# Gram and masked products of a gated delta rule: one matmul of 128 columns per unit in place of two of 64, from the fourth group on

## The chip, the cores and the metric

The kernel runs on one core of a Trainium2 chip. The metric is the device time of one execution in microseconds; the median of three runs before the change is 651.9 us (651.75 to 652.64). A core has a matrix engine (TensorE, in the profile PE, with its weight loads as PEld), a vector engine (VectorE, DVE), a scalar engine (ScalarE, ACT), GpSimd (POOL) and a queue for DMAs (SP). Matmul results go to PSUM, which the vector and scalar engines read.

## The reference

Two parts follow each other. The first is a delta rule with a state of 48 x 48 for each of 4 batches and 8 heads, over 768 tokens; the second is a gated MLP on its output, with 384 model and 1536 inner columns.

```
k_n = k / (norm(k) + 1e-06)
for t in range(S):
    y[t] = q[t] @ state
    v_old = k_n[t] @ state
    state = state + beta[t] * outer(k_n[t], v[t] - v_old)
x = y as (3072 tokens, 384)
out = (sigmoid(x @ w_gate) * (x @ w_val)) @ w_out
```

Taken in chunks of 64 tokens, the first part needs for each chunk and head the products of all its keys with one another (K by K, the Gram matrix, from which the norms and a triangular system come) and of its keys with its queries (K by Q, masked to the past).

## The kernel before

**Groups and units.** A group is one chunk of 64 tokens of all 4 batches, 256 tokens; there are N = 12 groups, 0 to 11. In a group there are 32 units, one per batch and head. A unit is named by `e` (which half of the 128 partitions holds its keys), `x` (which kind of two) and `j` (0 to 7). The tile `kqp[g % 2]` holds, in six sections, a group's K (sections 0 and 1 for the two kinds), its Q (2 to 4) and the masked products (the free halves of 2 and 4, and section 5). There are two such tiles, so group g's data is loaded over that of group g-2 (`load_group`, lines 122 to 126: four DMAs of K and Q, then those of V, K by tokens and beta).

**The two products.** `gram(g)` (lines 282 to 309) issues 32 matmuls of K by K (line 291): 48 rows, 64 stationary and 64 moving columns, into two PSUM tiles of one bank each, one per `e`. Ten ScalarE copies bring the result into G (line 303, six copies in another order of axes) and L (line 308, four copies). `masked(g)` (lines 311 to 327) issues 32 matmuls of K by Q (line 319) into two PSUM tiles, and four VectorE multiplications by a mask (line 324) write them back into `kqp`. The four units of one `j` lie in four different quarters of the array, by the rows of K and the columns of the output. All these PSUM tiles come from the pool `ps_aux`, which has two banks; the products `pu` of the updates (line 475), `yy` of the rows (lines 501 and 504) and the transposes `pt` (line 540) take turns in it with them.

**What follows.** `norms(g)` (from line 235) transposes G on VectorE and works out the norms; `solve(g)` (from line 329) solves the triangular systems in 66 VectorE steps; then `rest`, `updates` in three steps, `rows`, `advance` and `flip` take the group through the state and hand its output to the MLP. In the first three groups a shorter solve, `solve_halves`, is used, which takes both aux banks for a moment.

**The MLP.** For each group and each of 12 slices of the inner columns there is a gate block (`gate_val`, line 559: 18 matmuls of 256 columns), a sigmoid on ScalarE (line 564), a product on VectorE (line 565), a split into two numbers of lower precision (lines 570 and 575), and an output block two slices later (`outp`, line 590: 6 matmuls of 384 columns). Group 0 uses other forms of these (lines 556 and 584).

**The order of the work.** The order on every engine is the order in which the program issues it. It goes by slots, two to a slice and W = 24 to a group: an even slot has a gate block, an odd one an output block.

```
def slot(s):
    (odd: outp; even: gate_val)
    for fn in plan[s]: fn()
    (odd: split_hi; even: split_lo, gated)
    for fn in late[s]: fn()
    for fn in tail[s]: fn()
```

Lists `plan` and `late` hold what the first part does in a slot; `tail` holds the preparation of weights in the first 44 slots (ScalarE line 212, VectorE line 219). With w = 24 (g - 1), group g has its data loaded in `plan` of slot w-27; Gram in `late` of slot w-18 (`gram_later`, copies in the three slots after it: 4, 2, 4); the masked products in `late` of slot w-12 (`mask_later`, two masks in that slot, two at the head of the next); norms and solve over slots w-14 to w+8; `rest` at w+6; the updates at w+10, w+12 and w+14; `rows` and `advance` at w+16; the transposes at w+18. Group 3 has Gram at slot 32 and the masked products at 36. Counted modulo 24, a period of the steady part has `rest` and Gram in slot 6, the second update and the masked products in slot 12.

The counter `busy` is the planner's estimate of what VectorE has to do in a slot besides the solve: `spread` deals the steps of norms and solve to the slots by `max(0.1, 1.6 - busy[s])`. `mask_later` adds 1.4 to each of two slots.

Of the kernel before, what the change touches and what calls it, by code (L numbers as in the profile page):

```python
# [12 lines left out]
F32 = mybir.dt.float32  # L13
# [6 lines left out]
ALU = mybir.AluOpType  # L20
# [3 lines left out]
B, H, S, D = 4, 8, 768, 48  # L24
C = 64
# [5 lines left out]
J = 8  # L31
CP = 2 * J
NQ = 4 * CP
KINDS = [(e, x) for x in range(2) for e in range(2)]


def tokens_at(e, x):
    return 64 * e if x else 64 - 64 * e
# [17 lines left out]
def deltanet_gated_mlp(ctx: ExitStack, tc: tile.TileContext, kd, qd, kv, beta, words, out):  # L56
    nc = tc.nc
# [4 lines left out]
    wk = ctx.enter_context(tc.tile_pool(name="wk", bufs=1))  # L62
    ps_seq = ctx.enter_context(tc.tile_pool(name="ps_seq", bufs=2, space=PSUM))
    ps_aux = ctx.enter_context(tc.tile_pool(name="ps_aux", bufs=2, space=PSUM))
# [5 lines left out]
    kqp = [const.tile([128, 6, J, C], F32, name=f"kqp{i}") for i in range(2)]  # L70
# [3 lines left out]
    pmask = const.tile([128, 2, C], F32, name="pmask")  # L74
# [9 lines left out]
    state = [{} for _ in range(N)]  # L84
# [197 lines left out]
    def gram(g):  # L282

        kq, st = kqp[g % 2], state[g]
        st["G"] = G = wk.tile([128, 32, CP], F32, name=f"G_{g}", tag="G", bufs=1)
        st["L"] = L = wk.tile([128, CP, 32], F32, name=f"L_{g}", tag="L", bufs=2)
        pg = [ps_aux.tile([128, J, C], F32, name=f"pg_{g}_{e}", tag="aux") for e in range(2)]
        for j in range(J):
            for e, x in KINDS:
                r, t = 64 * e, tokens_at(e, x)  # L290
                nc.tensor.matmul(out=pg[e][t:t + 64, j], lhsT=kq[r:r + D, x, j], rhs=kq[r:r + D, x, j], start=True, stop=True)  # L291
        return blocks_of(pg, G, L, g == 0)
# [18 lines left out]
    def masked(g):  # L311

        kq = kqp[g % 2]
        pool, tag = (ps_aux, "aux") if g else (ps_out, "po")
        pp = [pool.tile([128, J, C], F32, name=f"pp_{g}_{e}", tag=tag) for e in range(2)]
        for j in range(J):
            for e, x in KINDS:
                r, t = 64 * e, tokens_at(e, x)
                nc.tensor.matmul(out=pp[e][t:t + 64, j], lhsT=kq[r:r + D, x, j], rhs=kq[r:r + D, 3 if x else 2 + 2 * e, j], start=True, stop=True)  # L319

        def masks():
            for e, x in sorted(KINDS):
                t, sec = tokens_at(e, x), 5 if x else 2 + 2 * e
                nc.vector.tensor_tensor(out=kq[t:t + 64, sec], in0=pp[e][t:t + 64],  # L324
                                        in1=pmask[t:t + 64, e].unsqueeze(1).to_broadcast([64, J, C]), op=ALU.mult)
                yield
        return masks()

    def solve(g):

        st = state[g]
        gp, gam = st["gp"], st["gam"]
        X = wk.tile([128, 16, 32], F32, name=f"X_{g}", tag="X", bufs=1)

        def scale(lo, hi):
            nc.vector.scalar_tensor_tensor(out=gp[:, lo:hi, 0:hi], in0=gp[:, lo:hi, 0:hi], scalar=-1.0,
                                           in1=gam[:, 0:hi].unsqueeze(1).to_broadcast([128, hi - lo, hi]), op0=ALU.mult, op1=ALU.mult)
        nc.vector.tensor_tensor(out=X, in0=dmask, in1=gam.unsqueeze(1).to_broadcast([128, 16, 32]), op=ALU.mult)
        yield
        scale(16, 32)  # L340
        yield
        scale(0, 16)
        yield
        for j in range(31, 0, -1):
            k, n = j // 2, 16 - j // 2
            tmp = wk.tile([128, n, j], F32, name=f"tmp_{g}_{j}", tag="tmp", bufs=2)
            nc.vector.tensor_tensor(out=tmp, in0=X[:, k:16, j:j + 1].to_broadcast([128, n, j]),  # L347
                                    in1=gp[:, j:j + 1, 0:j].to_broadcast([128, n, j]), op=ALU.mult)
            yield
            nc.vector.tensor_tensor(out=X[:, k:16, 0:j], in0=X[:, k:16, 0:j], in1=tmp, op=ALU.add)  # L350
            yield
        nc.vector.transpose(mt.rearrange("q c (k r) -> q k c r", r=2), X.rearrange("q k (c r) -> q k c r", r=2))
        yield
# [78 lines left out]
    def rest(g):  # L432

        st = state[g]
        kq, V = kqp[g % 2], st["kv"][:, 1]
        st["pk"] = pk = [ps_seq.tile([128, J, D], F32, name=f"pk_{g}_{e}", tag="seq") for e in range(2)]
        if g == 0:
            for e in range(2):
                nc.tensor.matmul(out=pk[e].rearrange("q j d -> q (j d)"), lhsT=flat[:, 0:128], rhs=su[:, 2].rearrange("q j d -> q (j d)").bitcast(BF16)[:, 0:J * D],
                                 start=True, stop=True, skip_group_check=True)  # L440
        for j in range(J if g else 0):
            for e, x in KINDS:
                r, t = 64 * e, tokens_at(e, x)
                nc.tensor.matmul(out=pk[e][t:t + 64, j], lhsT=kq[r:r + D, x, j], rhs=su[r:r + D, 2 if x else e, j],  # L444
                                 start=j == 0, stop=True, skip_group_check=True)
        if g == 0:
            st["R"] = [V[:, e * J:(e + 1) * J] for e in range(2)]
        else:
            st["R"] = [wk.tile([128, J, D], F32, name=f"R_{g}_{e}", tag="row", bufs=3) for e in range(2)]
            less(g)  # L450
# [61 lines left out]
    def advance(g):  # L512

        if g == N - 1:
            return
        Kt = state[g]["kv"][:, 0]
        if 1:
            pd = [ps_seq.tile([128, J, D], F32, name=f"pd_{g}_{t}", tag="seq") for t in range(2)]
            for j in range(J):
                for e, x in KINDS:  # L520
                    r, t = 64 * e, tokens_at(e, x)
                    nc.tensor.matmul(out=pd[t // 64][r:r + D, j], lhsT=Kt[t:t + 64, e * J + j], rhs=su[t:t + 64, 3 if x else e, j], start=True, stop=True)  # L522
            for e, x in KINDS:
                r, t = 64 * e, tokens_at(e, x)
                sl = su[r:r + D, 2 if x else e]
                if g == 0:
                    nc.scalar.copy(sl, pd[t // 64][r:r + D])
                else:
                    nc.vector.tensor_tensor(out=sl, in0=sl, in1=pd[t // 64][r:r + D], op=ALU.add)  # L529
# [73 lines left out]
    plan = collections.defaultdict(list)  # L603
    late = collections.defaultdict(list)

    def steps(gen, n=1):
        def fn():
            for _ in range(n):
                next(gen, None)
        return fn  # L610
# [14 lines left out]
    def take(gen, n=1):  # L625
        for _ in range(n):
            next(gen, None)
# [91 lines left out]
    busy = collections.Counter()  # L719

    def mask_later(g, s):
        def fn():
            masks = masked(g)
            take(masks, 2)
            plan[s + 1].insert(0, steps(masks, 2))
        late[s].append(fn)
        for i in range(2):
            busy[s + i] += 1.4

    def gram_later(g, s):  # L730
        def fn():
            copies = gram(g)
            for i, n in enumerate((4, 2, 4)):
                plan[s + 1 + i].append(steps(copies, n))
        late[s].append(fn)

    solves = []
    for g in range(N):
        w = W * (g - 1)
        if g == 0:  # L740
            late[3].append(lambda: advance(0))
            continue
        up, at_rows = (13, 19) if g < 3 else (10, 16)
        at_rest = {1: 8, 2: 28}.get(g, w + 6)
        late[at_rest].append(lambda g=g: rest(g))
        for step in range(3):
            late[w + up + 2 * step].append(lambda g=g, step=step: updates(g, step))
        late[w + at_rows].append(lambda g=g: rows(g))
        late[w + at_rows].append(lambda g=g: advance(g))
        for c in range(2):  # L750
            late[w + at_rows + 2].append(lambda g=g, c=c: flip(g, c))
            busy[w + at_rows + 2] += 0.6
        busy[at_rest] += 1.1
        busy[w + up + 2] += 1.1
        busy[w + at_rows] += 1.1
        busy[w + at_rows + 1] += 1.1
        if g == 1:
            mask_later(1, 11)
        else:
            if g > 2:  # L760
                plan[w - 27].append(lambda g=g: load_group(g))
            gram_later(g, {2: 3, 3: 32}.get(g, w - 18))
            mask_later(g, w + 1 if g == 2 else w - 12)
            if g > 2:
                solves.append((g, w - 13 if g == 3 else w - 14, w + 9))
            scaling(g, {2: 25, 3: 43}.get(g, w - 7))
# [77 lines left out]
```

## Time and profile before

| | |
|---|---|
| median of three runs | 651.9 us (651.75 to 652.64) |
| the profiled execution | 652.21 us, of which 650.5 us are the span from the first to the last instruction |
| mean granted TensorE clock | 0.991 |
| TensorE matmuls | 626.4 us busy (96%), 10556 records |
| VectorE | 467.9 us busy (72%), 1443 instructions |
| ScalarE | 321.2 us busy (49%), 870 instructions |
| DMA | 41.07 MB, mean 63 GB/s |

The shares are means over the whole span. The first 100 us, in which the weights are prepared and the first groups fill the pipeline, have gaps on TensorE; from about 150 us to 640 us TensorE runs without any. A matmul in fp32 shows as two records on TensorE, a pass each. The length of a record holds its way through the array, which overlaps the next record; what a burst costs is the distance from its first start to the first start of the work behind it.

### The profile page before, as it was taken

The page shows a single profiled execution, that of the slowest core. Times are in us where ns is not written, and L with a number is a line of the kernel's source. Part 1 is how long each engine was busy: PE and PEld are TensorE (multiplying, and loading weights), DVE is VectorE, ACT ScalarE, POOL GpSimd, SP SyncE. Part 2 cuts the span into 40 slices and gives each one's busy share as a digit, 9 for nine tenths or more (in the row PEclk, how much of TensorE's full clock was granted, in tenths as well). Part 3 has the DMA queues.
Part 4 walks back from the last instruction along what each step waited for, and adds up shares of the span by engine and source line. Part 5 has one row for each costly group of instructions (what it writes and reads, how often), then busy time and mean ns, then how long its engine had stood idle before and what let it go on. Part 6 is the DMA issues. An engine that isn't in the chain of part 4 may idle for free.

```text
span 650.5 us, 24072 instructions
## 1 busy us (share of the span) xinstructions
PE 626.4 (96%) x10556; PEld 585.0 (90%) x10556; DVE 467.9 (72%) x1443; ACT 321.2 (49%) x870; POOL 11.3 (2%) x30
## 2 busy tenths in 40 slices
PE   6788999799999999999999999999999999999996
PEld 4466778789999999999999999999999999999996
DVE  5887687568887977977967977977977977952221
ACT  5889385566455355355355355355355355334221
POOL 5000000000000000000000000000000000000000
PEclk9999799899999999999999999999999999999999
DMA  9597422201212103112102012113112100100101
GB/s 256 193 323 249 131 75 84 51 4 32 77 28 85 25 28 85 25 28 84 25 28 85 20 33 84 26 28 85 25 28 84 25 4 3 25 3 3 25 1 25
DMA packets 17769, 41.07 MB, mean 63 GB/s; under 512 B 4224, under 2 KB 7296, under 8 KB 17664
## 3 DMA queue, kind: packets, MB, share of 16 engines
q1 hardware_dynamic: 17664, 39.53, 21.1%
q8 instruction: 83, 1.36, 0.9%
q14 instruction: 22, 0.18, 0.1%
HBM read 34.80 MB, written 4.72 MB: 61 GB/s over the span
## 4 chain that ended last, share of the span: by engine, by line
PE 89%; DVE 5%; ACT 3%; issue 1%; DMA 1%; ACTq 0%; SPq 0%; DVEq 0%
PE gv L559 43%; PE po L590 22%; PE gv L556 4%; PE pu L475 3%; PE pg L291 2%; PE yy L501 2%; PE yy L504 2%; PE pp L319 2%; PE po L584 2%; PE pd L522 2%; PE pk L444 1%; PE pk L467 1%; PE pt L540 1%; ACT kv L279 1%; DVE kqp L324 1%
## 5 line engine op out<-in xcount | busy, mean ns | idle before, releaser
L559 PE MATMUL gv<-xx,w 128*128 128x256 f32 x2376 | 308.5, 284 | 0.0
L559 PEld LDWEIGHTS gv<-xx,w 128*128 128x128 f32 x2376 | 302.3, 191 | 0.9
L590 PE MATMUL po<-w,h 128*128 128x384 f32 x792 | 166.5, 345 | 0.0
L564 ACT ACTIVATE sg<-gv 128x256 f32<-128x256 f32 x144 | 55.3, 384 | 203.4 <-PE gv L559 190.6
L590 PEld LDWEIGHTS po<-w,h 128*128 128x128 f32 x792 | 133.3, 188 | 3.4 <-issue 0.3
L565 DVE TENSOR_TENSOR sg<-sg,gv 128x256 f32<-128x256 f32 x144 | 60.4, 419 | 85.2 <-ACT sg L564 84.7
L570 ACT CAST h<-sg 128x256 fp32r<-128x256 f32 x132 | 53.5, 405 | 53.0 <-DVE sg L565 51.6
L350 DVE TENSOR_TENSOR X<-X,tmp 128x126 f32<-128x126 f32 (+22 forms) x279 | 71.3, 256 | 8.9
L347 DVE TENSOR_TENSOR tmp<-X,gp 128x126 f32<-128x126 f32 (+22 forms) x279 | 71.0, 254 | 7.9
L575 DVE TENSOR_TENSOR h<-sg,h 128x256 fp32r<-128x256 f32 x132 | 55.1, 417 | 29.8 <-ACT h L570 29.8
L481 ACT COPY su<-pu 32x384 f32<-32x384 f32 x92 | 43.3, 471 | 15.2 <-PE pu L475 14.0
L279 ACT ACTIVATE kv<-kv,mq 128x48 f32<-128x48 f32 x192 | 48.1, 329 | 0.0
L556 PE MATMUL gv<-xx,u 128*128 128x256 f32 x144 | 35.8, 402 | 0.3 <-DVE xx L543 0.3
L529 DVE TENSOR_TENSOR su<-su,pd 48x384 f32<-48x384 f32 x40 | 22.1, 552 | 18.9 <-PE pd L522 18.4
L324 DVE TENSOR_TENSOR kqp<-pp,pmask 64x512 f32<-64x512 f32 x48 | 32.3, 687 | 3.4 <-PE pp L319 2.4
L303 ACT COPY G<-pg 32x256 f32<-32x256 f32 (+1 forms) x69 | 25.4, 368 | 18.6 <-PE pg L291 17.4
L556 PEld LDWEIGHTS gv<-xx,u 128*128 128x128 f32 x144 | 28.2, 201 | 5.5 <-ACT xx L543 0.8
L455 DVE TENSOR_TENSOR R<-kv,pk 128x384 f32<-128x384 f32 x44 | 22.4, 550 | 1.5 <-PE pk L444 1.5
L212 ACT CAST w<-u 128x384 fp32r<-128x384 f32 x36 | 18.2, 508 | 6.2 <-DVE w L219 5.9
L475 PEld LDWEIGHTS pu<-R,mt 32*32 32x32 f32 x1408 | 16.5, 105 | 4.9 <-issue 1.7
L219 DVE TENSOR_TENSOR w<-u,w 128x384 fp32r<-128x384 f32 x36 | 19.4, 550 | 1.5 <-ACT w L212 1.4
L475 PE MATMUL pu<-R,mt 32*32 32x48 f32 x1408 | 19.4, 202 | 0.9 <-DVE kqp L324 0.9
(104 smaller groups left out, 518.3 us busy)
## 6 DMA issues: line engine op xcount, KB each, us to landing
raw<-in_words_dram SPq DMA_DIRECT2D x36, 384.0 KB, 5.0
kv<-in_kv_dram SPq DMA_DIRECT2D x24, 384.0 KB, 5.0
kqp<-in_qd_dram SPq DMA_DIRECT2D x24, 256.0 KB, 4.2
kqp<-in_kd_dram SPq DMA_DIRECT2D x24, 192.0 KB, 3.6
out_dram<-ot SPq DMA_DIRECT2D x48, 96.0 KB, 2.2
beta<-in_beta_dram SPq DMA_DIRECT2D x12, 16.0 KB, 4.5
```

The lines of the kernel that those rows point to most:

```text
L279: nc.scalar.activation(V[:, c], V[:, c], AF.Copy, scale=mq[:, c, 0:1])
L347: nc.vector.tensor_tensor(out=tmp, in0=X[:, k:16, j:j + 1].to_broadcast([128, n, j]), in1=gp[:, j:j + 1, 0:j].to_broadcast([128, n, j]), o ...
L350: nc.vector.tensor_tensor(out=X[:, k:16, 0:j], in0=X[:, k:16, 0:j], in1=tmp, op=ALU.add)
L475: nc.tensor.matmul(out=pu[0 if g else x][r:r + 32, j], lhsT=mt[r:r + 32, e * J + j], rhs=R[e][r:r + 32, j], start=True, stop=True)
L481: nc.scalar.copy(su[r:r + 32, 3 if x else e], pu[0][r:r + 32])
L556: nc.tensor.matmul(out=pg[:, o], lhsT=parts[w, f][:, k * 128:(k + 1) * 128], rhs=x[0][:, k], start=k == 0, stop=k == KC - 1)
L559: nc.tensor.matmul(out=pg[:, o], lhsT=parts[w, f][:, a, k * 128:(k + 1) * 128], rhs=x[b][:, k], start=(k == 0 and q == 0), stop=(k == KC - ...
L564: nc.scalar.activation(h, st["gv", f][:, 0], AF.Sigmoid)
L565: nc.vector.tensor_tensor(out=h, in0=h, in1=st["gv", f][:, 1], op=ALU.mult)
L570: nc.scalar.copy(hh[:, 0], st["sg", f])
L575: nc.vector.tensor_tensor(out=hh[:, 1], in0=st["sg", f], in1=hh[:, 0].bitcast(F32), op=ALU.subtract)
L590: nc.tensor.matmul(out=po[s], lhsT=hh[:, a, ts], rhs=parts["o", f][:, w], start=(f == 0 and q == 0), stop=(f == NF - 1 and q == 2))
```

## The change

A new function `products(g, part)` takes the place of `gram(g)` and `masked(g)` for the groups 3 to 11. It works on half the units, `j` from 4 part to 4 part + 3. For each unit there is one matmul: K stays stationary, and the moving operand is K and Q of that unit side by side, 128 columns that are picked out of two sections of `kqp`. The result of 4 units, K by K and K by Q, fills one PSUM bank for each `e`, so a part takes both banks of `ps_aux`, as `gram` and `masked` each did. Copies and masks are the same in kind but work on half the units, so there are twenty copies and eight masks a group in place of ten and four.

`products_later(g, part, s)` puts a part's matmuls into `late[s]`, six copies and two masks into slot s+1 and four copies and two masks into slot s+2, the masks at the head of the slot's list. It adds 0.8 to `busy` of those two slots. For groups 4 to 11 the parts are at slots w-21 and w-18, for group 3 at slots 31 and 33.

```
+    def products(g, part):
+        kq, st, js = kqp[g % 2], state[g], slice(4 * part, 4 * part + 4)
+        if part == 0:
+            st["G"] = wk.tile([128, 32, CP], F32, name=f"G_{g}", tag="G", bufs=1)
+            st["L"] = wk.tile([128, CP, 32], F32, name=f"L_{g}", tag="L", bufs=2)
+        G, L = st["G"], st["L"]
+        both = [ps_aux.tile([128, 4, 2, C], F32, name=f"both_{g}_{part}_{e}", tag="aux") for e in range(2)]
+        for i in range(4):
+            j = 4 * part + i
+            for e, x in KINDS:
+                r, t, sec = 64 * e, tokens_at(e, x), 3 if x else 2 + 2 * e
+                nc.tensor.matmul(out=both[e][t:t + 64, i], lhsT=kq[r:r + D, x, j], rhs=kq[r:r + D, x:sec + 1:sec - x, j], start=True, stop=True)
+        def copies():
+            for e in range(2):
+                lo8 = e * J + 4 * part
+                for lo, hi, o in ((0, 128, 0), (32, 64, 32), (96, 128, 32)):
+                    nc.scalar.copy(G[lo:hi, :, lo8:lo8 + 4], both[e][lo:hi, :, 0, o:o + 32].rearrange("q p t -> q t p"))
+                    yield
+            for e in range(2):
+                lo8 = e * J + 4 * part
+                for t in (0, 64):
+                    lo, o = t + 32 * e, 32 - 32 * e
+                    nc.scalar.copy(L[lo:lo + 32, lo8:lo8 + 4], both[e][lo:lo + 32, :, 0, o:o + 32])
+                    yield
+        def masks():
+            for e, x in sorted(KINDS):
+                t, sec = tokens_at(e, x), 5 if x else 2 + 2 * e
+                nc.vector.tensor_tensor(out=kq[t:t + 64, sec, js], in0=both[e][t:t + 64, :, 1],
+                                        in1=pmask[t:t + 64, e].unsqueeze(1).to_broadcast([64, 4, C]), op=ALU.mult)
+                yield
+        return copies(), masks()
...
+    def products_later(g, part, s):
+        def fn():
+            copies, masks = products(g, part)
+            for i, n in enumerate((6, 4)):
+                plan[s + 1 + i].append(steps(copies, n))
+                plan[s + 1 + i].insert(0, steps(masks, 2))
+        late[s].append(fn)
+        for i in range(2):
+            busy[s + 1 + i] += 0.8
...
-            gram_later(g, {2: 3, 3: 32}.get(g, w - 18))
-            mask_later(g, w + 1 if g == 2 else w - 12)
+            if g == 2:
+                gram_later(g, 3)
+                mask_later(g, w + 1)
+            else:
+                for part, s in enumerate((31, 33) if g == 3 else (w - 21, w - 18)):
+                    products_later(g, part, s)
```

## The prediction

> **What bounds the kernel now.** I read the page's totals first, then the waits of TensorE, then the engines' busy time over one whole group, then TensorE's timeline around the two bursts that the change replaces.
>
> ```profile
> span 650.5 us, 24072 instructions
> PE 626.4 (96%) x10556; PEld 585.0 (90%) x10556; DVE 467.9 (72%) x1443; ACT 321.2 (49%) x870; POOL 11.3 (2%) x30
> ```
>
> ```profile
> PE pz L407 <- DVE mt L400: 3.4, 1, 3.4
> PE pu L475 <- DVE kqp L324: 0.9, 1, 0.9
> ```
>
> ```profile
> 299.40:348.36 48.96, 48.96 (x839) 47.80 (x838) 38.39 (x122) 22.68 (x64) 0.00 (x0) 1.00 0.17 46
> ```
>
> The second fence is what TensorE waited for from 104 to 640 us (us in total, times, longest): two waits, both before 150 us, beside one of 0.3. The third is one steady period of 24 slots (length, then PE, PEld, DVE, ACT and POOL busy, granted clock, DMA): TensorE has no gap in 48.96 us, VectorE is busy 38.39 us, ScalarE 22.68 us. So the time is the length of TensorE's instruction stream, and a term counts only if it shortens that stream or makes it wait. The next fence is that stream (start, length, engine, line, operation, count; the length of one row overlaps the next row, so costs are differences of starts).
>
> ```profile
> 268.32 2.33 PE L559 MATMUL gv<-xx,w 128*128 128x256 f32 x18
> 270.49 1.22 PE L590 MATMUL po<-w,h 128*128 128x384 f32 x6
> 271.54 2.33 PE L559 MATMUL gv<-xx,w 128*128 128x256 f32 x18
> ...
> 277.98 1.14 PE L291 MATMUL pg<-kqp 48*64 48x64 f32 x64
> 279.05 1.32 PE L590 MATMUL po<-w,h 128*128 128x384 f32 x6
> ...
> 290.69 1.16 PE L319 MATMUL pp<-kqp 48*64 48x64 f32 x64
> 291.78 1.33 PE L590 MATMUL po<-w,h 128*128 128x384 f32 x6
> 292.95 2.32 PE L559 MATMUL gv<-xx,w 128*128 128x256 f32 x18
> ...
> 296.01 1.31 PE L590 MATMUL po<-w,h 128*128 128x384 f32 x6
> 297.16 0.28 PE L559 MATMUL gv<-xx,w 128*128 128x256 f32 x1
> ```
>
> An undisturbed gate block takes 270.49 - 268.32 = 2.17 us, an output block 1.05. The Gram burst costs 279.05 - 277.98 = 1.07 (it follows the L444 burst directly), the masked burst 291.78 - 290.69 = 1.09. Each shows 64 records for 32 matmuls, two passes each.
>
> **The price of a 128-column matmul.** Four tiles of the array work at once, so records come in fours. The next rows are bursts cut by narrow windows at a four's start; the count says how many records are left.
>
> ```profile
> 290.79 1.05 PE L319 MATMUL pp<-kqp 48*64 48x64 f32 x60
> 291.38 0.47 PE L319 MATMUL pp<-kqp 48*64 48x64 f32 x20
> 277.11 1.05 PE L444 MATMUL pk<-su,kqp 48*64 48x48 f32 x60
> 277.69 0.47 PE L444 MATMUL pk<-su,kqp 48*64 48x48 f32 x20
> 285.74 0.82 PE L475 MATMUL pu<-R,mt 32*32 32x48 f32 x60
> 286.16 0.39 PE L475 MATMUL pu<-R,mt 32*32 32x48 f32 x20
> 305.75 0.82 PE L540 MATMUL pt<-ident,ys 128*128 128x128 f32 x6
> 306.29 0.27 PE L540 MATMUL pt<-ident,ys 128*128 128x128 f32 x1
> ```
>
> 40 records are ten fours: the step from four to four is 0.059 us for 64 weights and 64 columns (L319), 0.058 for 64 weights and 48 columns (L444), 0.042 for 32 weights and 48 columns (L475). With 64 weights the step doesn't follow the columns, so loading the weights sets it; with 32 weights it is 0.042/48 = 0.87 ns a column, near L540, whose five steps of 128 columns take (306.29 - 305.75)/5 = 0.108 us, 0.84 ns a column. So 64 columns need 0.054 us of streaming and now hide under 0.0585 of loading. Two matmuls of 64 columns cost a tile 0.117, one of 128 costs 0.108: doubling the columns saves almost nothing, because the removed weight loads had streaming under them all along. I take 0.109 per four; bounds 0.108 (streaming alone, L540) and 0.117 (no better than two of today's).
>
> A part has 16 matmuls, 32 records, 8 fours. Of the masked burst's 1.09 us, 15 steps are 0.88 and 0.21 is start and end. A part standing alone: 0.21 + 7 x 0.109 + 0.05 (its last four streams 64 columns longer) = 1.03 us. Right behind L444, from 1.07: 1.07 - 0.88 + 0.76 + 0.05 = 1.01.
>
> **The change, part by part, for groups 4 to 11.** *Removed:* the masked burst at slot w-12, 1.09, and 0.02 of a longer output block behind it (292.95 - 291.78 = 1.17 against 297.16 - 296.01 = 1.15 behind a small burst alone): -1.11 us. The lead-in and lead-out there stay, as the L467 burst before it stays. *Exchanged:* Gram at w-18 for part 1 behind L444: -0.06. *Added:* part 0 at w-21, an odd slot, where no small burst stands now; it goes between an output and a gate block. The first group has such places:
>
> ```profile
> 151.69 1.22 PE L590 MATMUL po<-w,h 128*128 128x384 f32 x6
> 152.84 0.88 PE L475 MATMUL pu<-R,mt 32*32 32x48 f32 x64
> ...
> 160.06 2.42 PE L559 MATMUL gv<-xx,w 128*128 128x256 f32 x18
> 162.32 1.22 PE L590 MATMUL po<-w,h 128*128 128x384 f32 x6
> ```
>
> The output block before a burst takes 1.15 instead of 1.05, the gate block behind one 2.26 instead of 2.17: 0.19 for a place of its own. Part 0 costs 1.03 + 0.19 = 1.22. Net 1.22 - 1.11 - 0.06 = +0.05 a group, +0.4 over eight.
>
> *ScalarE and VectorE.* Ten PSUM copies of 256 elements a partition become twenty of 128, four masks of 512 become eight of 256.
>
> ```profile
> L308 ACT COPY L<-pg 32x256 f32<-32x256 f32 x48 | 17.4, 362 | 0.6
> L324 DVE TENSOR_TENSOR kqp<-pp,pmask 64x512 f32<-64x512 f32 x48 | 32.3, 687 | 3.4 <-PE pp L319 2.4
> ```
>
> A half copy costs between 0.18 (half of 362 ns) and 0.36; I take 0.28, so +2.0 us of ScalarE a group. A half mask costs between 0.34 and 0.69; 0.42, as L565 below on 256 elements, so +0.6 of VectorE. Both lie beside TensorE, under 26 and 10 us of idle time a period. Uncovered they would be 9 x 0.6 = 5 us (VectorE) or 18 us (ScalarE). The masks' waits move from slot w-12 to the starts of w-20, w-19, w-17 and w-16, where solve steps and the gate product L565 queue behind them; today four masks run back to back (2.7 us) and TensorE doesn't wait. The solve steps are dealt out again by the planner's room, with the same last slot.
>
> *Queues and buffers.* Moved bursts issue no DMA, and none is issued elsewhere. Part 0 needs Q nine slots earlier than the masked burst did:
>
> ```profile
> 301.20 1.14 SPq L109 DMA_DIRECT2D kqp<-in_qd_dram  x2
> ```
> ```profile
> kqp<-in_qd_dram SPq DMA_DIRECT2D x24, 256.0 KB, 4.2
> ```
>
> Q of a group is issued when the rows of two groups before are done (301.20) and lands 4 us later; part 0 stands one period after 271.54, near 320.5, 14 us later. Slots w-21 and w-18 have three slots between them for part 0's ten copies and four masks to free the two aux banks. So nothing here.
>
> **Group 3**, whose slots are tight, has terms of its own.
>
> ```profile
> 133.16 1.16 PE L291 MATMUL pg<-kqp 48*64 48x64 f32 x64
> ...
> 140.89 1.41 PE L319 MATMUL pp<-kqp 48*64 48x64 f32 x64
> 142.23 1.32 PE L590 MATMUL po<-w,h 128*128 128x384 f32 x6
> 144.43 0.88 PE L475 MATMUL pu<-R,mt 32*32 32x48 f32 x64 [0.88 <-DVE kqp L324]
> ```
> ```profile
> 139.59 1.50 ACT L308 COPY L<-pg 32x256 f32<-32x256 f32 x4
> ```
> ```profile
> 133.27 0.38 ACT L564 ACTIVATE sg<-gv 128x256 f32<-128x256 f32 x1 [2.72 <-PE gv L559]
> 133.55 0.51 ACT L212 CAST w<-u 128x384 fp32r<-128x384 f32 x1
> ```
> ```profile
> 133.69 0.42 DVE L565 TENSOR_TENSOR sg<-sg,gv 128x256 f32<-128x256 f32 x1 [2.33 <-ACT sg L564]
> 134.02 1.02 DVE L219 TENSOR_TENSOR w<-u,w 128x384 fp32r<-128x384 f32 x2
> ```
>
> Its masked burst took 1.34 instead of 1.09, since the L308 copies held the second bank until 141.09; and L475 came 2.20 behind the output block's start instead of 1.15, since masks held its bank. Both stalls, 0.25 + 1.05 = 1.30, go. But part 1 at slot 33 comes one output block behind part 0's last copies and masks. From the sigmoid's start (0.11 after the gate block's end, 133.16): ScalarE is through sigmoid and weight cast at +0.79 and through four L copies at +1.9; VectorE ends L565 at +0.84, one L219 at +1.35, two masks at +2.2. TensorE arrives at -0.11 + 1.15 = +1.04. New stall 1.15 (bounds 0.6 without that L219, 1.7 with two). Both bursts of group 3 stood alone before and do after: 2 x -0.06. In all -1.30 + 1.15 - 0.12 = -0.3.
>
> **Sum.** +0.4 - 0.3 = +0.1 us on the profiled execution's own 652.21 (span 650.5). The median of the runs is 651.9, 0.3 under it, so 652.0.
>
> **Rivals.**
> *The weight loads don't hide behind the longer stream (slower).* The first step of every burst speaks for it: 290.69 to 290.79 is 0.10, load plus stream in a row. Against it: from the second four on the step is 0.059, less than load plus stream, at three shapes. If every step were serial, 0.108 + 0.0585 = 0.167, the 18 parts gain 7 steps x 0.058 each, 7.3 us: 659.3. The Trainium skill, "TensorE: Matmul & The Clock Gate", Part 3, says that a weight load overlaps running matmuls only where the row group differs, which would make this case the rule; by it today's steps would be 0.112 as well, and this trace shows 0.059.
> *Part 1 waits for aux banks in every group (slower).* Place: slot w-18. Part 0's readers have about 2.26 + 1.05 + 2.26 + 1 = 6.5 us; VectorE, 78% busy, needs 1.7 of them for masks, ScalarE 2.8 for copies. It decides once VectorE runs over 3 us late there; for it speaks how full VectorE is, against it that today's 2.7 us of masks delays nobody. Half to a whole output block eight times is 4 to 8 us: 656 to 660.
> *The moving operand in two pieces costs extra, or runs as two streams of 64.* No burst here moves two separate pieces. As two of today's steps (0.117): 126 steps x 0.008 = 1.0 us, 653.0; with 7 ns more, 654.
> *The bursts are paid by matmuls, not columns (faster).* Then the four stays at 0.0585 and a part saves 7 x 0.05 = 0.35: 18 parts, 6.4 us, 645.6. L475 and L540, both near 0.85 ns a column, speak against it.
> *Group 3's new stall doesn't come*, say because its masks run before the weight differences: -1.15, 650.8.
>
> **How the numbers follow.** This kernel's runs tell 0.2%, 1.3 us, from no change. Forecast 0.70 (its own errors: 0.008 us on 126 steps, 0.6 on the stall, a few fetch gaps; of it 0.05 faster, 0.56 same, 0.09 slower). Serial loads 0.04, aux banks 0.09, both slower. Two pieces 0.07, 0.04 of it slower. Paid by matmuls 0.04, faster. No stall 0.06, half of it faster. Sums: faster 0.12, same 0.62, slower 0.26. The range goes from 650.4, under the missing stall, to 655.2, over the two pieces; outside lie most of the aux rival, serial loads and paid by matmuls, 0.16.
>
> **What would show it.** Right: x32 bursts of 128 columns, 1.03 us to the next start, at a step near 0.109; the isolated one lengthening its neighbours by 0.19; a period still near 48.9 us; one wait of some 1.1 us near 136 us, that at 144 gone. Wrong: a step of 0.167 or 0.06, or waits of TensorE on copies or masks in every period.

## The result and the profile after

The change makes the kernel slower: 660.25 us median (659.43 to 661.82, four runs) against 652.2 (four runs), a ratio of 1.0126 with a 95% interval of 1.0111 to 1.0142. The forecast was 652.0 with a range of 650.4 to 655.2. The profiled execution took 661.02 us with a span of 659.3, 8.8 us above the span before.

The page of the kernel after the change, its totals and the groups of the new lines (L341 the merged matmuls, L347 and L353 the copies to G and L, L359 the masks):

```profile
span 659.3 us, 23031 instructions
PE 629.1 (95%) x9972; PEld 584.4 (89%) x9980; DVE 472.6 (72%) x1479; ACT 334.7 (51%) x960; POOL 11.3 (2%) x30
...
L347 ACT COPY G<-both 32x128 f32<-32x128 f32 (+1 forms) x108 | 28.2, 261 | 39.8 <-DVE kqp L359 25.8
...
L359 DVE TENSOR_TENSOR kqp<-both,pmask 64x256 f32<-64x256 f32 x72 | 30.3, 421 | 13.4 <-ACT G L347 10.3
```

A half copy takes 261 ns (0.28 was taken), a half mask 421 (0.42). New is what stands behind the last bar: copies that stood idle 25.8 us for masks, and masks that stood idle 10.3 us for copies. A mask writes into `kqp` and a copy into G, so neither needs the other's result; they read the same PSUM tile, which fills one bank. First the steady part, TensorE's timeline of the changed kernel in slots 3 to 7 of a late group (the second fence is the same burst from its second four on, and from its sixth):

```profile
327.70 1.22 PE L625 MATMUL po<-w,h 128*128 128x384 f32 x6
328.85 1.10 PE L341 MATMUL both<-kqp 48*64 48x128 f32 x32
329.89 2.41 PE L594 MATMUL gv<-xx,w 128*128 128x256 f32 x18
332.14 1.22 PE L625 MATMUL po<-w,h 128*128 128x384 f32 x6
333.19 2.32 PE L594 MATMUL gv<-xx,w 128*128 128x256 f32 x18
335.45 1.15 PE L479 MATMUL pk<-su,kqp 48*64 48x48 f32 x64
336.42 1.25 PE L341 MATMUL both<-kqp 48*64 48x128 f32 x32
337.60 0.62 PE L625 MATMUL po<-w,h 128*128 128x384 f32 x2
```
```profile
329.01 0.94 PE L341 MATMUL both<-kqp 48*64 48x128 f32 x28
...
329.45 0.51 PE L341 MATMUL both<-kqp 48*64 48x128 f32 x12
```

16 records, four fours, from 329.01 to 329.45: a step of 0.110 us. Part 0 takes 329.89 - 328.85 = 1.04, the output block before it 1.15 and the gate block behind it 2.25. Part 1 behind L479 takes 337.60 - 336.42 = 1.18. One period of this kernel (from the output block of slot 113 to that of slot 137) beside the same one before:

```profile
310.86:359.87 49.01, 49.01 (x783) 47.39 (x775) 38.84 (x126) 24.20 (x75) 0.00 (x0) 1.00 0.17 45
```
```profile
302.42:351.37 48.95, 48.95 (x846) 47.80 (x838) 38.39 (x122) 22.68 (x65) 0.00 (x0) 1.00 0.17 46
```

49.01 against 48.95: the steady groups do not hold the 8 us. (From slot 65 on, seven periods of the kernel before take 48.77 to 49.33; the shortest is the least disturbed.) Group 3's stage holds most of them. TensorE there, after the change:

```profile
129.99 1.31 PE L625 MATMUL po<-w,h 128*128 128x384 f32 x6
131.23 1.10 PE L341 MATMUL both<-kqp 48*64 48x128 f32 x32
132.47 2.31 PE L594 MATMUL gv<-xx,w 128*128 128x256 f32 x18
134.62 1.22 PE L625 MATMUL po<-w,h 128*128 128x384 f32 x6
136.28 0.43 PE L341 MATMUL both<-kqp 48*64 48x128 f32 x2 [0.44 <-ACT L L353]
137.71 1.10 PE L341 MATMUL both<-kqp 48*64 48x128 f32 x30 [1.00 <-ACT L L353]
138.74 3.92 PE L594 MATMUL gv<-xx,w 128*128 128x256 f32 x18
142.50 1.21 PE L625 MATMUL po<-w,h 128*128 128x384 f32 x6
```

ScalarE and VectorE in the same stretch, in this order:

```profile
133.33 1.67 ACT L347 COPY G<-both 128x128 f32<-128x128 f32 x6 [2.54 <-DVE kqp L359]
...
135.71 0.52 ACT L353 COPY L<-both 32x128 f32<-32x128 f32 x2
137.13 0.53 ACT L353 COPY L<-both 32x128 f32<-32x128 f32 x2 [0.91 <-DVE kqp L359]
```
```profile
132.38 0.86 DVE L359 TENSOR_TENSOR kqp<-both,pmask 64x256 f32<-64x256 f32 x2 [1.12 <-PE both L341]
...
135.78 0.55 DVE L219 TENSOR_TENSOR w<-u,w 128x384 fp32r<-128x384 f32 x1
136.25 0.85 DVE L359 TENSOR_TENSOR kqp<-both,pmask 64x256 f32<-64x256 f32 x2
```

Part 0 is done by 132.4. The six G copies start at 133.33, behind the two masks of the bank that the first three of them read. The last two L copies start at 137.13, behind the second pair of masks, though two copies of the other bank were through at 136.23. Part 1 gets its first records at 136.28 and the others at 137.71. The gate block behind it then takes 142.50 - 138.74 = 3.76 us in place of 2.25, since TensorE's granted clock (the third number from the end) is 0.55 in it:

```profile
138.74:142.50 3.76, 3.76 (x22) 3.76 (x19) 1.18 (x3) 1.56 (x6) 0.00 (x0) 0.55 0.01 2
```

And it goes on: of TensorE's waits from 104 to 650 us, new or longer ones are

```profile
PE both L341 <- ACT L L353: 2.4, 3, 1.0
PE pd L557 <- issue: 1.5, 2, 0.9
PE pu L510 <- DVE R L490: 0.9, 2, 0.7
```

To find where a kernel loses, its starts are compared with those of the kernel before at the same blocks. "Stage" is from the output block of slot 31 to that of slot 45, where group 3's parts and, behind them, group 2's updates and rows lie (32.57 us before), "group 4" from there to slot 63 (35.90), "rest" from there to the last output block (443.75). The first column is the start of slot 31's output block, up to which all these kernels issue the same work.

| kernel | slot 31 | stage | group 4 | rest | median |
|---|---|---|---|---|---|
| before | 129.75 | 32.57 | 35.90 | 443.75 | 652.2 |
| after | 129.99 | +5.65 | +1.45 | +1.45 | 660.25 |
| group 3 separate | 132.59 | +0.71 | +2.12 | +0.53 | 656.59 |
| group 3 alone merged | 129.06 | +4.66 | -0.08 | -0.21 | 656.1 |
| banks turned | 129.20 | +3.72 | +0.33 | -0.01 | 655.65 |
| old places | 128.85 | 0.00 | +0.89 | +12.70 | 664.74 |
| old dealing | 129.66 | +3.83 | +2.46 | +1.25 | 660.53 |
| banks turned, old dealing | 129.25 | +2.34 | +1.27 | +0.47 | 655.87 |
| banks turned, group 3 separate | 130.75 | +0.71 | +0.79 | -0.86 | 652.67 |
| banks turned, old places | 128.22 | 0.00 | +0.77 | +11.43 | 664.94 |
| banks turned, part 1 at 34 | 129.65 | +1.51 | +0.37 | +0.42 | 654.3 |
| the same, old dealing | 129.05 | +1.46 | +1.29 | -0.03 | 654.34 |

The columns are from one profiled execution each, the median from several runs. The first column scatters by 4.4 us with no cause in the program; the mean granted clock up to there is 0.99 in the earliest kernel (128.22) and 0.92 in the latest (132.59), 0.95 or 0.96 in the others. So the medians, too, say less of a us or two than the stage does. Nor is the stage free of other causes: it is 0.71 longer in the two kernels with merged bursts at slots w-21 and w-18 whose group 3 is as before, 0.60 of it at the L536 burst. A program cause is possible there: group 4's parts add to the planner's counter at slots over which group 3's solve is dealt.

### The profile page after: what moved, and what is told of

It is laid out like the page before. It is cut to its first block, busy times and chain, and to the rows that moved or that the text cites. A ratio compares the mean times of both kernels' runs of the same rounds, so it can differ in the third digit from the quotient of the medians.

```text
span 659.3 us, 23031 instructions
## 1 busy us (share of the span) xinstructions
PE 629.1 (95%) x9972; PEld 584.4 (89%) x9980; DVE 472.6 (72%) x1479; ACT 334.7 (51%) x960; POOL 11.3 (2%) x30
## 4 chain that ended last, share of the span: by engine, by line
PE 82%; DVE 10%; ACT 4%; DMA 2%; issue 1%; ACTq 0%; SPq 0%; DVEq 0%
PE gv L594 40%; PE po L625 21%; PE gv L591 3%; PE pu L510 3%; PE both L341 3%; PE yy L536 2%; PE yy L539 2%; PE po L619 2%; PE pd L557 1%; PE pk L479 1%; PE pk L502 1%; DMA raw<-in_words_dram 1%; PE pt L575 1%; DVE sg L600 1%; DVE w L219 1%
## 5 line engine op out<-in xcount | busy, mean ns | idle before, releaser
L516 ACT COPY su<-pu 32x384 f32<-32x384 f32 x92 | 43.3, 471 | 11.6 <-PE pu L510 10.3
L347 ACT COPY G<-both 32x128 f32<-32x128 f32 (+1 forms) x108 | 28.2, 261 | 39.8 <-DVE kqp L359 25.8
L359 DVE TENSOR_TENSOR kqp<-both,pmask 64x256 f32<-64x256 f32 x72 | 30.3, 421 | 13.4 <-ACT G L347 10.3
L341 PE MATMUL both<-kqp 48*64 48x128 f32 x576 | 21.8, 275 | 2.4 <-ACT L L353 2.4
L353 ACT COPY L<-both 32x128 f32<-32x128 f32 x72 | 18.4, 255 | 8.8 <-DVE kqp L359 8.0
L490 DVE TENSOR_TENSOR R<-kv,pk 128x384 f32<-128x384 f32 x44 | 22.3, 549 | 0.2 <-PE pk L479 0.2
L341 PEld LDWEIGHTS both<-kqp 48*64 48x64 f32 x576 | 17.2, 133 | 5.5 <-ACT L L353 3.2
```

What stands on the lines that cost most here:

```text
L341: nc.tensor.matmul(out=both[e][t:t + 64, i], lhsT=kq[r:r + D, x, j], rhs=kq[r:r + D, x:sec + 1:sec - x, j], start=True, stop=True)
L516: nc.scalar.copy(su[r:r + 32, 3 if x else e], pu[0][r:r + 32])
```

## The experiments

**Group 3 separate, groups 4 to 11 merged.**

```
-            if g == 2:
-                gram_later(g, 3)
-                mask_later(g, w + 1)
+            if g < 4:
+                gram_later(g, {2: 3, 3: 32}[g])
+                mask_later(g, w + 1 if g == 2 else w - 12)
             else:
-                for part, s in enumerate((31, 33) if g == 3 else (w - 21, w - 18)):
+                for part, s in enumerate((w - 21, w - 18)):
```

> Group 3 keeps two separate bursts at slots 32 and 36; groups 4 to 11 have the merged ones. Theory A (the loss is made once, where group 3's parts meet the preparation of the weights; the trace after the change shows TensorE's starts falling back 5.7 us between 130 and 166 us, 1.3 us at group 4's part 1, and 0.2 us in each later group): 652.2 + 8 x 0.2 = 653.8, or 655.1 if group 4's wait stays; no wait of TensorE on a copy near 136 us. Theory B (each merged group costs the same, 8 us over 9 groups): 652.2 + 8 x 0.9 = 659.3.

Measured 656.59, 1.0065 of before (1.004 to 1.0091), the stage +0.71. Theory A gains: one group of nine takes 3.7 of the 8 us with it. The median lies 1.5 us over A's upper value; this kernel's profile was 2.8 us late before slot 31, where nothing differs, and group 4's wait stayed (0.9 us).

**Only group 3 merged.** The edit is the converse: `products_later` at slots 31 and 33 for group 3, `gram_later` at w-18 and `mask_later` at w-12 for groups 4 to 11.

> The other half: only group 3 has the merged bursts at slots 31 and 33, groups 4 to 11 have two separate ones. Theory A: 652.2 + 5.7 = 657.9, with TensorE's clock showing a drop near 139 us; 656.3 where that drop, 1.6 us, doesn't come. Theory B: 652.2 + 0.9 = 653.1.

Measured 656.1, 1.0061 (1.0041 to 1.0081): the stage +4.66, the clock's drop there as in the kernel after, and nothing behind it (-0.08 and -0.21). That is 1.8 us under A's value, although the clock's drop came, and 3 over B's. B falls with it: one group can't cost half of the loss if all cost the same. The losses of the two halves, 4.4 and 3.9 us, add up to 8.3 against 8.05 for the whole.

**Banks turned.** Copies and masks are issued so that ScalarE and VectorE read different banks at a time: the masks take the second bank first, and in slot s+2 the copies stand ahead of the masks. In both slots the copies also move from the end of the slot's list to its head.

```
-            for e, x in sorted(KINDS):
+            for e, x in sorted(KINDS, reverse=True):
...
-                plan[s + 1 + i].append(steps(copies, n))
-                plan[s + 1 + i].insert(0, steps(masks, 2))
+                order = [steps(masks, 2), steps(copies, n)]
+                plan[s + 1 + i][:0] = order[::-1] if i else order
```

> As after the change, but ScalarE's copies and VectorE's masks are issued so that they turn to different banks: in the slot after a part the masks of the second bank and the copies of G, first bank first; in the next slot the copies of L first and then the masks of the first bank. Theory C (ScalarE and VectorE take turns at one bank, and part 1 of groups 3 and 4 waits for the last L copies because those stand behind masks of their bank): these copies start some 0.9 us earlier, TensorE's waits of 1.0 us at part 1 of groups 3 and 4 shrink to about 0.4, and with what follows from them 660.3 becomes 657.5 to 659. If the turns don't matter (only the late masks do): 660, waits as they are.

Measured 655.65, 1.0059 (1.0036 to 1.0082), 4.6 us less than after the change, more than the 1.3 to 2.8 expected. ScalarE's and TensorE's timelines in group 3's stage:

```profile
131.61 0.82 ACT L347 COPY G<-both 128x128 f32<-128x128 f32 x3 [1.72 <-PE both L341]
132.60 0.82 ACT L347 COPY G<-both 128x128 f32<-128x128 f32 x3 [0.17 <-DVE kqp L359]
...
134.64 1.06 ACT L353 COPY L<-both 32x128 f32<-32x128 f32 x4
```
```profile
133.75 1.22 PE L625 MATMUL po<-w,h 128*128 128x384 f32 x6
135.75 1.44 PE L341 MATMUL both<-kqp 48*64 48x128 f32 x32 [0.78 <-ACT L L353]
137.13 2.42 PE L594 MATMUL gv<-xx,w 128*128 128x256 f32 x18
139.38 0.34 PE L625 MATMUL po<-w,h 128*128 128x384 f32 x1
```

The first three G copies now wait for TensorE, not for a mask; the four L copies run in one piece; part 1 starts 2.00 us after its output block and takes 1.38, where after the change these were 1.66 and 2.46; and the gate block behind it takes 2.25: the clock doesn't drop. No data, no bank and no instruction was changed, only the order of issue; and in this stage the traces show the instructions of ScalarE, VectorE and TensorE in exactly the order that they have after the change, line by line; what differs is the bank that a mask reads. Theory C holds: readers of one bank on two engines take turns, in the order of the program. (One tile fills one bank here, so the runs do not tell a bank from a tile.) By the table, the stage gave 1.9 of these us, of which the clock's drop is 1.5, group 4 gave 1.1 and the later groups 1.5. The Trainium skill, "PSUM — Partial Sum Buffer", section "PSUM bank collisions raise a hardware error", says that two engines must not touch the same bank and quadrant at once, two readers included, and that the compiler therefore orders them. The waits in these traces agree that the two are kept apart, but they go by the whole bank: after the change, the L copy of rows 32 to 63 at 137.13 had its own rows' mask done at 136.66 and still waited for the mask of rows 64 to 127. What would happen without the order, no run here shows.

**Merged bursts at the old places**, slots w-18 and w-12, so that none stands alone, with norms and solve from w-10 on in place of w-14 and the scaling of V at w-4; group 3 separate.

> Merged bursts of groups 4 to 11 at the two places of the separate ones, slots w-18 and w-12, both behind another small burst; norms and solve start at w-10 in place of w-14, the scaling of V at w-4; group 3 keeps separate bursts. Theory of the prediction's terms: a burst with a place of its own costs 0.19, and none has one here; part 0 behind L444 costs 1.18 as in the trace after the change, part 1 behind L467 1.03, against 1.07 and 1.11 before: 652.2 + 8 x 0.03 = 652.4. If the denser norms and solve make TensorE wait, 654 and more, with waits on VectorE in every period.

Measured 664.74, 1.0186 (1.0163 to 1.0209): with its variant below, the slowest of all. TensorE's waits (us in total, times, longest) and a piece of its timeline:

```profile
PE pu L510 <- DVE mt L387: 9.3, 8, 1.2
PE pu L510 <- ACT L L353: 2.8, 8, 0.6
```
```profile
293.94 1.10 PE L341 MATMUL both<-kqp 48*64 48x128 f32 x32
294.97 1.32 PE L625 MATMUL po<-w,h 128*128 128x384 f32 x6
```

The bursts cost no more than was expected (part 1 behind L502 takes 294.97 - 293.94 = 1.03, part 0 behind L479 1.01 in place of 1.18), but the first update waits in each of eight groups for the solve's last step, which VectorE reaches up to 1.2 us too late, and the second update waits for the L copies.

**The planner's old dealing.** The counter keeps the 1.4 for slots 36 and 37, so that group 3's norms and solve are dealt to the slots as before the change.

```
     for at in (29, 30, 30, 31):
         plan[at].append(steps(halves2))
+    for s in (36, 37):
+        busy[s] += 1.4
```

> As after the change, but the planner's counter of VectorE work keeps the 1.4 that it had for slots 36 and 37, so that group 3's norms and solve are dealt out as before the change. Theory D (part of group 3's loss comes from the dealing: without that 1.4 more steps of norms and solve stand ahead of the subtraction for R of the second update, and the third update's matmuls wait for it): TensorE's wait on R near 156 us (0.9 us) goes, the delays between 150 and 165 us shrink, 1.5 to 3 us of 660.3 come back, 657 to 659. If the dealing doesn't matter, 660 with that wait as it is.

Measured 660.53, 1.0143 (1.0118 to 1.0169): nothing gained, though the wait on R went and the stage fell from +5.65 to +3.83. One us of that came back in group 4 (+2.46 in place of +1.45), where part 1 again stood behind copies and masks. As a cause of the 8 us theory D falls; it moves work between two waits. Of the stage's delay behind the first update it is a cause all the same: 1.65 us were lost there, where after the change it was 3.47.

**Banks turned and the old dealing.**

> Both: copies and masks turned to different banks (655.65 by itself) and group 3's norms and solve dealt out as before the change. If theories C and D are separate causes, the two gains add: 655.65 - 1.5 to 3 = 652.7 to 654.2, group 3's part between 129 and 166 us then costs 1 to 2 us more than before in place of 3.7. If both cure the same wait, 655.5.

Measured 655.87, 1.0061 (1.0043 to 1.008). The gains don't add: the stage is 1.4 us shorter than with banks turned alone, group 4 0.9 longer.

**Banks turned, group 3 separate:** the merged matmul in the steady part by itself.

> Copies and masks turned to different banks, groups 4 to 11 merged, group 3 with separate bursts as before: the merged matmul by itself in the steady part. The prediction's terms: part 0 1.03 + 0.19, part 1 1.00, against 1.11 and 1.07 before, +0.04 to +0.05 a group: +0.4 over eight groups, 652.6, inside 0.2% of 652.2; no wait of TensorE on copies or masks after 150 us. If waits stay in the steady part, 654 to 656.

Measured 652.67 over twelve runs, 1.0018 (1.0005 to 1.0032). TensorE around part 1, and all its waits from 150 to 640 us:

```profile
329.32 1.15 PE L479 MATMUL pk<-su,kqp 48*64 48x48 f32 x64
330.29 1.07 PE L341 MATMUL both<-kqp 48*64 48x128 f32 x32
331.29 1.31 PE L625 MATMUL po<-w,h 128*128 128x384 f32 x6
```
```profile
PE yy L536 <- ACT su L516: 0.3, 1, 0.3
PE both L341 <- ACT L L353: 0.3, 1, 0.3
```

Part 1 takes 331.29 - 330.29 = 1.00 in place of the 1.18 after the change, so those 0.18 us a group were the late masks of part 0, not the place. The same period as above, which repeats from group to group here:

```profile
304.73:353.53 48.80, 48.80 (x782) 47.19 (x775) 38.87 (x126) 24.20 (x75) 0.00 (x0) 1.00 0.17 46
```

48.80 is 0.03 over the shortest period of the kernel before, 48.77, where the sum said 0.05. (The -0.86 in the table is no gain of the merged matmul: three of the seven periods before were 0.18 to 0.56 over 48.77.) The steady part costs what the sum said, and there is nothing in the merged matmul for TensorE to win.

**Banks turned at the old places.**

> Merged bursts at the places of the separate ones with copies and masks turned to different banks. In the first kernel with these places (664.7) the last step of the solve came 1.2 us late in every group, behind the late norms and behind a copy and a mask that took turns at a bank, and the first update waited for it. If the turns make that delay, most of 12 us goes: 653 to 656. If the solve that starts four slots later makes it (VectorE has too little time), 660 to 664 with the wait on the solve as long as it was.

Measured 664.94, 1.0199 (1.0176 to 1.0222). The wait on the L copies went, that on the solve stayed at 10.4 us over eight groups, the longest 1.4: the turns do not make it, and the later start of norms and solve is the cause that is left, though the later scaling of V came with it and was not tried alone.

**Part 1 of group 3 one slot later**, with banks turned: `(31, 34)` in place of `(31, 33)`.

> Copies and masks turned to different banks (655.65 by itself) and group 3's part 1 one slot later, at 34 in place of 33, behind the gate block. Theory E (the rest of group 3's cost, 3.7 us between the output blocks of slots 31 and 45, comes from part 1 standing one output block behind part 0's readers): its wait of 0.8 us goes and with it the delays behind it, the stretch costs 1 to 2 us more than before, 653 to 654. Theory F (VectorE and ScalarE are late in this stage with the preparation of the weights, whatever the parts do): the wait goes, but the updates and rows behind it wait longer, the stretch still costs 3 us, 655 to 656.

Measured 654.3, 1.0031 (1.0018 to 1.0043). TensorE's timeline there:

```profile
135.33 2.32 PE L594 MATMUL gv<-xx,w 128*128 128x256 f32 x18
137.58 1.10 PE L341 MATMUL both<-kqp 48*64 48x128 f32 x32
138.62 1.31 PE L625 MATMUL po<-w,h 128*128 128x384 f32 x6
```

Part 1 starts right behind the gate block, 2.25 us after that block's start, and takes 1.04. The stage is +1.51, in theory E's range; F's 3 us don't come. The time itself lies between the two. So the place of part 1, one output block behind part 0's readers, held another 2.2 us of the stage.

**The same with the old dealing.**

> The same with group 3's norms and solve dealt out as before the change (the planner's 1.4 kept in slots 36 and 37; with part 1 at 33 this took the stretch from 3.7 to 2.3 us). Theory E: 0 to 1 us for the stretch, 652.5 to 653.5. Theory F: 2 us or more, 654 to 656.

Measured 654.34, 1.0031 (1.0012 to 1.0049), the stage +1.46: above E's value and below F's, while the time lies in F's range. The dealing makes no difference to the stage (+1.51 without it) once the wait at part 1 is gone.

What is left of the stage, 1.5 us, is not settled: in both of these kernels TensorE shows issue waits inside the L557 burst (0.4 us in the stage with part 1 at 34, 0.6 later; the kernel before has one of 0.3, near 547 us) and waits of the L536 burst on copies of the update (0.9). Half of it need not come from group 3's bursts at all: 0.71 stands in the table where group 3 is separate, too. No version here beats the kernel before.

## Why the prediction was wrong

**The forecast fell in the paragraph on group 3:** at the size of the term "New stall 1.15", and at "In all -1.30 + 1.15 - 0.12 = -0.3", which ends at the first update and puts all behind the stall at nothing. The stage cost +5.65. Its parts, from the differences of starts after and before: TensorE reached part 1 0.51 us late (the output block at 134.62 took 1.66 in place of 1.15) and then waited 1.43 inside it, 1.9 in place of 1.15. That alone is over the upper bound of 1.7, for a reason that the working left out: it let ScalarE's four L copies end at +1.9 and VectorE's masks at +2.2 side by side, where the last two copies came behind the masks. The two things after it were priced at nothing. The clock dropped in the next gate block: 1.5 us. And the update bursts from 149 to 166 us came late by 3.5 us together, by the same differences (0.67 at L502, 1.24 around the third update, 0.41 at the rows, 1.15 at L557). The old stalls of 1.30 did go.

The kernel with banks turned parts the two errors. There the engines do work side by side, part 1 costs 2.00 + 1.38 - 1.15 - 1.03 = 1.20 in place of 1.15, the clock doesn't drop, and TensorE stands at -0.13 us against before when it reaches the first update: the -0.3 was nearly right as far as it went. The stage still costs +3.72, so 3.85 us are lost in the update bursts behind. The stall alone doesn't make them late either: with part 1 at 34 there is no stall, the first update comes 1.09 us earlier than before, and the stage ends 1.51 later. In these bursts TensorE waits for ScalarE's copies (L516), for VectorE's subtraction (L490) and in issue waits at L557; with part 1 at 34, what it had gained ahead of them it lost again there. Part of that is the planner's dealing of the solve, which the prediction named and gave no price: 1.8 us of the 3.5 went with the old dealing, 1.4 with banks turned as well, next to none with part 1 at 34. What the rest comes from stays open.

Outside the stage the change lost 1.45 us in group 4, where part 1 waited 0.95 us behind the masks, and 1.45 in the later groups.

**The rival "Part 1 waits for aux banks in every group"** had the right wait and the right sign, at a chance of 0.09. That its size fits (4 to 8 us; 8.05 measured) is luck: it adds half to a whole output block eight times, where long waits came in groups 3 and 4 alone, the later groups lost 0.18 us each at part 1, and most of the 8 us is what followed in group 3's stage. Its condition, VectorE over 3 us late, is not what decided: with banks turned (655.65) VectorE has the same work, and TensorE no longer waits at group 4's part 1. The turns at a bank weren't seen by the working: the lines of the change that put both masks and copies of one bank into the same slot were read as two engines side by side.

**The price of a 128-column matmul was right.** Taken 0.109 a four, measured 0.110; a part alone 1.03, measured 1.04; part 1 behind the small burst 1.01, measured 1.00 once nothing waited; a place of its own 0.19, measured 0.10 before and 0.08 behind. The kernel with banks turned and group 3 separate, which has these terms without group 3's, stands at 1.0018 (1.0005 to 1.0032) where they give 1.0006, and its period is 0.03 longer where they give 0.05. The rival with serial loads, 659.3, is near the measured time and is wrong all the same: its step of 0.167 isn't in the trace. The rule of the Trainium skill beside it ("TensorE: Matmul & The Clock Gate", Part 3), that a weight load hides only where the row group differs, doesn't agree with the kernel after either. The next weights of a tile go to the row group in which its own matmul runs; in a row the two would make a step of 0.167, and it is 0.110. "Paid by matmuls" and "two pieces" fall with the step of 0.110.

**Covers.** VectorE's and ScalarE's extra work was given as hidden, with 5 and 18 us if uncovered. The work is hidden in the steady part (38.84 and 24.20 us busy in 49.01). What wasn't hidden is the order between the two, which busy times don't show.

**The missing stall** (650.8) asked for masks ahead of the weight differences; masks ahead of copies were the trouble.

## What to carry to other kernels

When one matmul puts two results into one PSUM bank and two engines read them, count these reads in a row, in the program's order, not side by side: let the engines start at different banks (results in banks of their own might do as well; no run here tried that). Ask of a matmul that is to be merged what sets its step today; where the weight load hides streaming of nearly the same length, halving the loads wins almost nothing (0.117 against 0.110 here). And in the tightest stage of a kernel, here the first groups, don't sum the stalls that go and come as if each ended where it stands: follow TensorE through the bursts behind them and ask what other engines these wait for.

## What the runs showed of the hardware that was not expected

Readers on two engines of one PSUM bank took turns even where their bytes, and their rows, were different: 25.8 us of ScalarE's and 10.3 us of VectorE's idle time after the change at the G copies and the masks, of which TensorE felt little (2.4 us of its own waits).

In the three kernels in which part 1 of group 3 waited behind the masks (after, old dealing, group 3 alone merged), some 1.4 us in two pieces, the gate block right behind ran at about half the clock, 1.5 us lost; in those with banks turned, with one wait of 0.8 us there or less, none did. The length of the wait doesn't decide alone: with the old dealing, group 4's part 1 waited 0.93 and 0.95 us, and with banks turned at the old places the first updates waited up to 1.4 us in one piece, and the clock stayed at 1.00. In every trace here the granted clock changes at moments a whole number of steps of 3.41 us apart (after the change it is 0.50 from 138.86 to 142.27), so where a wait lies in these steps may matter; no run was made to test it.

The time before the change under test isn't constant: the start of slot 31's output block lay between 128.22 and 132.59 us in twelve kernels that issue the same work up to there. The order goes roughly with the granted clock up to that block (0.99 at 128.22, 0.92 at 132.59). A us or two of a median can come from there, and a comparison by the same blocks of two traces leaves it out.
